# Mixed expert units with the weights stationary: first layer of a full tile and a half tile as one moving operand of 384 columns

## The chip, the cores and the metric

The kernel runs on one core of a Trainium2 chip. The metric is the device time of one execution in microseconds; the time of a kernel is the median of its runs. Engines are named as in the profile: PE is TensorE (PEld its weight loads), DVE VectorE, ACT ScalarE, POOL GpSimd, SP SyncE.

## What is computed

Three blocks follow one another: an attention over clusters of heads, a dense feed-forward block, and a block of 8 experts, all in float32. Only the last is touched by the change:

```
out = x.copy()
do_compute = (x @ w_skip) > 0                  # x: 1536 x 512
e = argmax(x[do_compute] @ w_gate)             # one expert of 8 per token
for e in range(8):
    h = maximum(x[rows of e] @ w1[e], 0)       # w1[e]: 512 x 1024
    y[rows of e] = gate * (h @ w2[e])          # w2[e]: 1024 x 512
out[do_compute] = x + y
```

## The kernel before

Every float32 operand of a matmul is split in two parts, a high one (a cast to fp32r) and a low one (the operand less its high part). A product is three matmuls: high by high, high by low, and low by high. All matmuls in question accumulate in PSUM over the 512 rows of `w1` in four steps `k` of 128, and over the columns of `w1` in two chunks `c` of 512.

The expert block, `moe2`, works through a fixed list of units, the string `TURNS = "01U2UZUVWV"`, numbered 0 to 9; a unit is the tokens that one expert takes at a time. U is two full tiles of 128 tokens, W one full tile, Z and the digits 1 and 2 one half tile of 64, and V one full tile and one half tile, 192 tokens in all. Units 7 and 9 are V, unit 8 between them is W. A section for more units than these stands behind a branch that these inputs don't take.

Per unit the work is this. `gather` brings the tokens' rows by an indirect DMA; `transx` (lines 1233 to 1246) turns them on PE into PSUM tiles `pt`, and ACT and DVE make the high and the low part of `xT`. `first(t, c)` (line 1269) makes 512 columns of the hidden layer for tile `t`. For the units U it calls `wide`, which keeps the weights stationary and lets 256 tokens move, so that the hidden layer comes out already turned. For all other units the tokens are stationary and 512 weight columns move (`group`, line 1202): 12 matmuls of 128x512 for a full tile, 8 for a half tile, whose high and low parts share one stationary operand of 128 columns. The result `h` (two PSUM buffers in the pool of that name) is read out by ACT into `hb` (line 1279), turned back by PE in `transh` (line 1300 for a full tile, line 1296 with the matrix `two`, which also adds the two halves, for a half tile), and split again by ACT and DVE into `hT`. `second` multiplies `hT` by `w2`, into `yo`.

The weights of a unit are four chunks of 128x2048, loaded by DMA into `raw` or `even`; `ahead` takes one of five slots (`wh` and `wl`, `lasth` and `lastl`) as soon as its last reader is done, casts the chunk on ACT (`hi`, line 1541) and subtracts on DVE (`lo`, line 1545). The order of all this is that of the Python code: each engine takes its instructions in the order in which `run` emits them. `run` walks a list of turns `(t, c)`: all first layers of a unit, then its second layers. Before a one-tile unit's second layer one first layer of the next unit is put. In a turn, `ahead` stands in front of the matmuls, and the `transh` of one turn comes after the matmuls of the next; for the units U (`w`), `transh` follows at once and `ahead` comes after it.

Of the kernel before, what the change touches and what calls it, by code (L numbers as in the profile page):

```python
# [20 lines left out]
P = 128  # L21
# [1158 lines left out]
def moe2(ctx, tc, A, cst, R, y1d, wsp, wk, op, ps, x0, route, room):  # L1180
# [6 lines left out]
    xs = x0[1][2]  # L1187
# [24 lines left out]

    left = {(n, c): len(u) for n, u in enumerate(UNIT) for c in range(NPC)}
# [6 lines left out]
    def is_half(t):  # L1220
        return TILES[t][2] < P
# [4 lines left out]

    def side(t):
        return slice(UNIT[TILES[t][0]].index(t) * P, (UNIT[TILES[t][0]].index(t) + 1) * P)
# [4 lines left out]
    def transx(t):  # L1233
        n = TILES[t][0]
        pt = ps["t"].tile([P, 4, P], F32, tag="t", name="pt")
        if is_half(t):
            xT[t] = [xs]
            transpose_half(nc, ident, xg[t], pt, xs, TILES[t][1])
            return
        if is_wide(n):  # L1240
            if t == UNIT[n][0]:
                xT[n, "wide"] = [both("xT", 2) for _ in "hl"]
            xT[t] = [x[:, :, side(t)] for x in xT[n, "wide"]]
        else:
            x = both("xT", 2)
            xT[t] = x[:, :, :P], x[:, :, P:]
        transpose_x(nc, ident, xg[t], pt, *xT[t])
# [20 lines left out]

    def first(t, c, ks=range(4)):
        n = TILES[t][0]  # L1270
        if is_wide(n):
            return wide(t, c)
        if ks[0] == 0:
            hp[t, c] = ps["h"].tile([P, DM], F32, tag="h", name="h")
        group(hp[t, c], xT[t], wsp.w[n, c], is_half(t), True, True, ks)
        if ks[-1] == KD - 1:
            done(n, c)
            r = wk.tile([P, DM], F32, tag="hb", name="hb")
            nc.scalar.activation(r, hp.pop((t, c)), AF.Copy if is_half(t) else AF.Relu)
            hb[t, c] = r  # L1280

    def transh(t, c, late=None):
        r = hb.pop((t, c))
        if is_wide(TILES[t][0]):
            return r()
# [28 lines left out]
    def second(t, c, which=range(3)):  # L1314
        n = TILES[t][0]
        if c == 0 and which[0] == 0:
            yo[t] = ps["y"].tile([P, DM], F32, tag="y", name="yo")
# [98 lines left out]
    def run(n0, n1, fresh=False):  # L1416
# [40 lines left out]
        for t, c in turns:  # L1457
            n = TILES[t][0]
            w = c < 2 and is_wide(n)
# [16 lines left out]
            if c < 2 and n + 1 < n1:  # L1476

                if len(tiles[n]) == 1:
                    rows = tiles[n + 1] if is_wide(n + 1) and c == 0 else () if is_wide(n + 1) else tiles[n + 1][c:c + 1]
# [69 lines left out]
def kernel(ctx, tc, A):  # L1549
# [169 lines left out]
    def more():  # L1719
# [10 lines left out]
        def last():  # L1730
# [4 lines left out]
            return (xT[:, 0], xT[:, 1]), *(x[1][:, o:o + 4 * P].rearrange("p (k m) -> p k m", k=DM // P) for o in (2048, 2048 + 4 * P))  # L1735
# [90 lines left out]
```

## Time and profile before

| | us |
|---|---|
| runs shown, median of 3 | 719.35 (719.34, 719.35, 721.04) |
| profiled execution, its own time | 718.92 |
| its span, first to last instruction | 717.1 |
| first matmul of unit 7 | 652.84 |
| first matmul of unit 8 | 674.56 |
| last matmul's start group, then the last output and its scatter | 707.80, 708.93, 709.96 |

The profile is one execution on the chip. A busy share is an average over the whole span; what a change in one stage is worth is read in that stage's timeline. There, a row is a run of like instructions of one engine: when it begins, how long it is busy, how many there are, and in brackets how long the engine was idle before and who ended that. Consecutive matmuls overlap, so their cost is taken from one start to the next and not from the busy time. The rows themselves are in the section ahead of the prediction.

### The profile page before, as it was taken

The numbers are of one execution on the slowest core, as the hardware profiler recorded it, in microseconds if no ns is written. First come the engines' busy times: TensorE is split into PE (matmuls) and PEld (weight loads), VectorE is DVE, ScalarE is ACT, GpSimd is POOL, SyncE is SP. The second block draws the span as 40 slices with busy tenths as digits, with TensorE's granted clock in tenths as the row PEclk, the third lists the DMA queues.
The fourth block names the chain that finished last, engine by engine and source line by source line (L and its number), as shares of the span: only waits on it lengthen the run. The fifth ranks groups of instructions, "written<-read, shape, count | busy, mean of one in ns | idle before, by whom it ended". The sixth has DMA issues, their size and how long they took to land.

```text
span 717.1 us, 11778 instructions
## 1 busy us (share of the span) xinstructions
PE 699.9 (98%) x4111; PEld 625.8 (87%) x4111; DVE 568.2 (79%) x1114; ACT 472.1 (66%) x905; POOL 381.9 (53%) x339
## 2 busy tenths in 40 slices
PE   8999999999999999999999999999999999999995
PEld 5998989989999899888889999999888989898884
DVE  6989988898989878788784989976468888785651
ACT  6889788888889954554545655556645867574640
POOL 4659779697896386666662000001025888884201
PEclk9999999999999999999999999999999999999998
DMA  7867666676765133333203600026444999996000
GB/s 204 213 160 177 133 166 157 156 173 127 169 164 123 41 115 122 133 138 136 119 1 122 188 0 1 1 64 202 147 149 139 385 367 320 353 352 262 33 10 25
DMA packets 43904, 108.42 MB, mean 151 GB/s; under 512 B 8698, under 2 KB 24522, under 8 KB 38464
## 3 DMA queue, kind: packets, MB, share of 16 engines
q1 hardware_dynamic: 36768, 67.03, 34.4%
q0 software_dynamic: 7072, 40.60, 15.3%
q8 instruction: 34, 0.56, 0.3%
q14 instruction: 30, 0.25, 0.1%
HBM read 74.78 MB, written 10.10 MB: 118 GB/s over the span
## 4 chain that ended last, share of the span: by engine, by line
PE 66%; DVE 8%; DMA 8%; ACT 6%; POOL 6%; issue 5%; POOLq 0%; SPq 0%; ACTq 0%; DVEq 0%
PE h L677 18%; PE y L726 16%; DMA raw<-in_wall_dram,wi 7%; PE yo L1210 5%; PE pt L342 4%; PE hw L1263 4%; PE h L1210 3%; PE s L308 2%; PE px L360 2%; DVE nm L324 2%; PE y L736 2%; ACT e L331 2%; PE s L311 2%; DVE etl L345 2%; PE px L362 2%
## 5 line engine op out<-in xcount | busy, mean ns | idle before, releaser
L345 DVE TENSOR_TENSOR etl<-pt,eth 128x384 fp32r<-128x384 f32 x192 | 101.9, 549 | 19.6 <-ACT eth L344 18.4
L344 ACT CAST eth<-pt 128x384 fp32r<-128x384 f32 x192 | 90.9, 485 | 19.4 <-PE pt L342 19.4
L1177 POOL DMA_INDIRECT xg<-y1d,gi x16 | 27.8, 1738 | 130.5 <-DVE gi L1026 113.8
L342 PE MATMUL pt<-ident,e 128*128 128x128 f32 x576 | 93.8, 272 | 0.3 <-ACT e L331 0.3
L331 ACT ACTIVATE e<-s,nm 128x768 f32<-128x768 f32 x96 | 87.4, 910 | 6.4 <-DVE nm L324 5.6
L324 DVE TENSOR_REDUCE nm<-s 128x1 f32<-128x768 f32 x96 | 90.5, 943 | 0.9 <-PE s L311 0.8
L705 ACT CAST gh<-gm 128x384 fp32r<-128x384 f32 x60 | 30.8, 513 | 81.8 <-DVE gm L703 58.5
L342 PEld LDWEIGHTS pt<-ident,e 128*128 128x128 f32 x576 | 73.6, 140 | 7.0 <-ACT e L331 0.6
L707 DVE TENSOR_TENSOR gl<-gm,gh 128x384 fp32r<-128x384 f32 x60 | 49.4, 824 | 25.7 <-ACT gh L705 25.7
L360 PE MATMUL px<-etl,vh 128*64 128x384 f32 (+1 forms) x192 | 65.5, 368 | 1.5 <-DVE etl L345 1.3
L308 PE MATMUL s<-AB 128*128 128x384 f32 x192 | 57.5, 381 | 2.5 <-ACT e L331 2.1
L577 POOL TENSOR_TENSOR pre<-ct,pre 128x512 int32<-128x512 int32 x26 | 37.2, 1451 | 35.8 <-DVE ct L575 35.8
L677 PE MATMUL h<-xh,wh 128*128 128x384 f32 x256 | 55.6, 338 | 0.6 <-DVE gm L700 0.4
L677 PE MATMUL h<-xh,wl 128*128 128x384 f32 x256 | 56.0, 339 | 0.0
L677 PE MATMUL h<-xl,wh 128*128 128x384 f32 x256 | 55.0, 336 | 0.0
L362 PE MATMUL px<-eth,vh 128*128 128x384 f32 x160 | 54.0, 337 | 0.0
L1545 DVE TENSOR_TENSOR wl<-raw,wh 128x2048 fp32r<-128x2048 f32 (+2 forms) x26 | 44.5, 1717 | 11.7 <-ACT wh L1541 11.7
L311 PE MATMUL s<-CD 128*128 128x384 f32 x192 | 49.3, 338 | 1.0 <-DVE CD L439 1.0
L677 PEld LDWEIGHTS h<-xh,wh 128*128 128x128 f32 x256 | 45.5, 188 | 3.3 <-DVE gm L700 0.5
L677 PEld LDWEIGHTS h<-xh,wl 128*128 128x128 f32 x256 | 44.6, 188 | 2.7 <-POOL wl L649 2.6
L677 PEld LDWEIGHTS h<-xl,wh 128*128 128x128 f32 x256 | 45.7, 188 | 0.0
L1541 ACT CAST wh<-raw 128x2048 fp32r<-128x2048 f32 (+2 forms) x26 | 37.4, 1444 | 10.6 <-PE yo L1210 10.6
(357 smaller groups left out, 1816.8 us busy)
## 6 DMA issues: line engine op xcount, KB each, us to landing
AB<-RL SPq DMA_DIRECT2D x31, 384.0 KB, 5.3
raw<-in_w_in_dram SPq DMA_DIRECT2D x16, 512.0 KB, 4.0
raw<-in_w_out_dram SPq DMA_DIRECT2D x16, 512.0 KB, 4.7
raw<-in_wall_dram SPq DMA_DIRECT2D x8, 1024.0 KB, 8.2
Tp<-in_qkT_dram SPq DMA_DIRECT2D x16, 384.0 KB, 4.1
CD<-RL SPq DMA_DIRECT2D x15, 384.0 KB, 6.9
raw<-in_wall_dram POOLq DMA_DIRECT2D x4, 1024.0 KB, 11.8
vt<-in_v_dram SPq DMA_DIRECT2D x8, 384.0 KB, 6.3
```

Of the source, the lines that this page charges most:

```text
L308: nc.tensor.matmul(s[:, u, :384], lhsT=AB[:, 0, t * P:(t + 1) * P], rhs=AB[:, 1, ks], start=True, stop=False)
L311: nc.tensor.matmul(s[:, u, :384], lhsT=CD[:, 0, t * P:(t + 1) * P], rhs=CD[:, 1, ks], start=False, stop=True)
L324: nc.vector.tensor_reduce(out=nm, in_=s[:, :, :384], axis=AX.XY, op=ALU.max, negate=True)
L331: nc.scalar.activation(e.rearrange("p (u c) -> p u c", u=2), s[:, :, :384], AF.Exp, bias=nm, accum_out=den[:, i % 3:i % 3 + 1])
L342: nc.tensor.transpose(pt[:, i2], e[:, kt * P:(kt + 1) * P], ident)
L344: nc.scalar.copy(eh, pt)
L345: lows[u] = lambda: nc.vector.tensor_tensor(out=etl[:, 3 * u:3 * u + 3, q * P:(q + 1) * P], in0=pt, in1=eh.bitcast(F32), op=ALU.subtract)
L360: nc.tensor.matmul(px[:m], lhsT=vh[:, kt, :m], rhs=etl[:, kt], start=False, stop=False)
L362: nc.tensor.matmul(px, lhsT=vh[:, kt, :], rhs=eth[:, kt], start=False, stop=(kt == NT - 1))
L677: nc.tensor.matmul(hs[c], lhsT=a[:, k * P:(k + 1) * P], rhs=x[:, k, c * HC:(c + 1) * HC], start=(k == 0 and i == 0), stop=(k == KD - 1 and ...
L726: nc.tensor.matmul(ys[gi * GT + t], lhsT=a[:, t * P:(t + 1) * P], rhs=w, start=(f == 0 and n == 0), stop=(gi == 0 and f == NF - 1 and n == 2))
L1210: nc.tensor.matmul(out, lhsT=l[:, k], rhs=r[:, k * DM:(k + 1) * DM], start=start and k == 0 and i == 0, stop=stop and k == 3 and i == len( ...
```

## The change

For units of a full tile and a half tile (`is_mid`: units 7 and 9; unit 0 is left as it is) the first layer is done like that of the units U, by a new function `middle`: the weights are stationary, 128 columns at a time, and the 192 tokens move. The moving operand `xm` holds, for each `k`, 384 columns: 192 high ones (128 of the full tile, 64 of the half one) and then 192 low ones. The high weights meet all 384, the low weights meet the first 256, that is the 192 high ones and 64 of the low ones. In PSUM, columns 0 to 191 so gather high by high and low by high, columns 192 to 383 high by low. ACT copies the second half out (`r`), DVE adds the first half to it (`q`), ACT takes the Relu as the high part, and DVE makes the low parts, laid out in `hm` so that the half tile's high and low part lie side by side for `second`. One call of `middle` makes 256 columns of the hidden layer for all 192 tokens, in two PSUM tiles of 128 columns (`d`), from the pool `h` with its two buffers; a unit takes four calls where it took four calls of `group` before. `transh` makes no PE instruction any more for these units.

`run` treats them like the units U: `transh` follows at once, `ahead` comes behind it, and behind unit 8's first turn both tiles of unit 9 are turned together. `last` gives `xm` a place in the tiles `lasth` and `lastl`, over that of `xs`.

```
@@ moe2 @@
+    class Parts:
+        def __init__(self, m, half, low):
+            o = P if half else 4 * HALF * low
+            self.m, self.s = m, slice(o, o + P)
+        def __getitem__(self, at):
+            k = at[1]
+            return self.m[k // 2][:, k % 2, self.s]
...
+    def is_mid(n):
+        return len(UNIT[n]) == 2 and not is_wide(n) and n > 1
@@ transx @@
+        if is_mid(n):
+            for k in range(KD):
+                nc.tensor.transpose(pt[:, k], xg[t][:, k * P:(k + 1) * P], ident)
+            a, m, b0 = (P, HALF, TILES[t][1]) if is_half(t) else (0, P, 0)
+            for i, x in enumerate(xm):
+                hi, lo, p2 = x[:, :, a:a + m], x[:, :, 3 * HALF + a:3 * HALF + a + m], pt[:, 2 * i:2 * i + 2, b0:b0 + m]
+                nc.scalar.copy(hi, p2)
+                nc.vector.tensor_tensor(out=lo, in0=p2, in1=hi.bitcast(F32), op=ALU.subtract)
+            return
...
+    def middle(t, c):
+        n = TILES[t][0]
+        wh, wl = wsp.w[n, c]
+        i = UNIT[n].index(t)
+        H3 = 3 * HALF
+        hm = both("hT", HT).rearrange("p a b -> p (a b)")[:, :12 * HALF].rearrange("p (d m) -> p d m", d=2)
+        hM.setdefault((n, c), {})[i] = hm
+        r, q = (wk.tile([P, DM], F32, tag="hb", name="hb")[:, :2 * H3].rearrange("p (d m) -> p d m", d=2) for _ in range(2))
+        for d in range(2):
+            h = ps["h"].tile([P, DM], F32, tag="h", name="hm")
+            for k in range(4):
+                o, x = k * DM + (2 * i + d) * P, xm[k // 2][:, k % 2]
+                if k == 3:
+                    nc.tensor.matmul(h[:, :4 * HALF], lhsT=wl[:, o:o + P], rhs=x[:, :4 * HALF], start=False, stop=False)
+                nc.tensor.matmul(h[:, :6 * HALF], lhsT=wh[:, o:o + P], rhs=x, start=k == 0, stop=k == 3)
+                if k < 3:
+                    nc.tensor.matmul(h[:, :4 * HALF], lhsT=wl[:, o:o + P], rhs=x[:, :4 * HALF], start=False, stop=False)
+            nc.scalar.copy(r[:, d], h[:, H3:2 * H3])
+            nc.vector.tensor_tensor(out=q[:, d], in0=h[:, :H3], in1=r[:, d], op=ALU.add)
+        done(n, c)
+        def parts():
+            nc.scalar.activation(hm[:, :, :H3], q, AF.Relu)
+            for a, b, m in ((0, 4 * HALF, P), (P, H3, HALF)):
+                nc.vector.scalar_tensor_tensor(out=hm[:, :, b:b + m], in0=q[:, :, a:a + m], scalar=0.0, in1=hm[:, :, a:a + m].bitcast(F32),
+                                               op0=ALU.max, op1=ALU.subtract)
+        hb[t, c] = parts
...
@@ transh @@
-        if is_wide(TILES[t][0]):
+        if is_wide(TILES[t][0]) or is_mid(TILES[t][0]):
             return r()
@@ second @@
+        if is_mid(n):
+            hT[t, c] = Parts(hM[n, c], is_half(t), 0), Parts(hM[n, c], is_half(t), 1)
...
@@ run @@
-            w = c < 2 and is_wide(n)
+            w = c < 2 and (is_wide(n) or is_mid(n))
...
-                    rows = tiles[n + 1] if is_wide(n + 1) and c == 0 else () if is_wide(n + 1) else tiles[n + 1][c:c + 1]
+                    w1 = is_wide(n + 1) or is_mid(n + 1)
+                    rows = tiles[n + 1] if w1 and c == 0 else () if w1 else tiles[n + 1][c:c + 1]
...
@@ last @@
+            mid = [t[:, 2048:2048 + 6 * P].rearrange("p (k m) -> p k m", k=2) for t in x]
```

On PE, where unit 7 begins, the tokens were stationary (the second name of each pair; `h_7789` is the full tile's PSUM buffer, `h_7804` the half tile's, `lasth` and `lastl` a weight slot's two parts, which also house the tokens' parts), with the turning `pt` behind them:

```order
L1210 MATMUL h_7789<-lasth_6289,xT_7712 128x512 [waits Activation_49]
L1210 MATMUL h_7789<-lasth_6289,xT_7712 128x512 x3
L1210 MATMUL h_7789<-lastl_6290,xT_7712 128x512 x4
L1210 MATMUL h_7789<-lasth_6289,xT_7712 128x512 [waits DVE_49]
L1210 MATMUL h_7789<-lasth_6289,xT_7712 128x512 x3
L1210 MATMUL h_7804<-lasth_6289,lastl_6290 128x512 [waits DVE_49]
L1210 MATMUL h_7804<-lasth_6289,lastl_6290 128x512 x3
L1210 MATMUL h_7804<-lastl_6290 128x512 x4
L1300 MATMUL pt_7815<-ident_63,hb_7802 128x128 [waits Activation_49]
L1300 MATMUL pt_7815<-ident_63,hb_7802 128x128 x3
```

Now it is this, from the fourth PSUM tile of unit 7 into the fifth; `hm_7834` is in the second of the two buffers, `hm_7856` in the first again:

```order
L1309 MATMUL hm_7834<-lasth_6289 128x384 [waits DVE_49]
L1311 MATMUL hm_7834<-lasth_6289,lastl_6290 128x256
L1309 MATMUL hm_7834<-lasth_6289 128x384
L1311 MATMUL hm_7834<-lasth_6289,lastl_6290 128x256
L1309 MATMUL hm_7834<-lastl_6290,lasth_6289 128x384
L1311 MATMUL hm_7834<-lastl_6290 128x256
L1308 MATMUL hm_7834<-lastl_6290 128x256
L1309 MATMUL hm_7834<-lastl_6290,lasth_6289 128x384
L1309 MATMUL hm_7856<-lasth_6289,wh2_6286 128x384 [waits DVE_49]
L1311 MATMUL hm_7856<-lasth_6289,wl2_6287 128x256
```

Eight matmuls of 384 and 256 columns stand for each PSUM tile, no turning is left, and each new tile waits for DVE, since DVE's add is the last reader of the buffer that it takes over.

On ACT in unit 7, the casts of unit 8's first two weight chunks (`even0`, `even1`) stood here, ahead of the reads of `h` and behind the second of them:

```order
L1541 CAST wh4_6537<-even0_5265 128x2048 [waits DMASW1_49,DVE_49,PE_49]
L1279 ACTIVATE hb_7802<-h_7789 128x512 [waits PE_49]
L1279 ACTIVATE hb_7813<-h_7804 128x512 [waits PE_49]
L1301 CAST hT_7816<-pt_7815 128x4x128 [waits DVE_49,PE_49]
L1541 CAST lasth_6289<-even1_6288 128x2048 [waits DMASW7_49,DVE_49]
L1279 ACTIVATE hb_7841<-h_7828 128x512 [waits PE_49,Activation_49]
L1297 ACTIVATE hT_7844<-pt_7843 128x4x64 [waits PE_49]
L1279 ACTIVATE hb_7860<-h_7851 128x512 [waits PE_49,Activation_49]
L1301 CAST hT_7863<-pt_7862 128x4x128 [waits DVE_49,PE_49]
```

They now stand between the calls of `middle`, each behind one call's Relu (line 1317) and ahead of the next call's two copies (line 1312):

```order
L1312 COPY hb_7791<-hm_7793 128x192 [waits PE_49]
L1312 COPY hb_7791<-hm_7804 128x192 [waits PE_49]
L1317 ACTIVATE hT_7790<-hb_7792 128x2x192 [waits DVE_49]
L1600 CAST wh4_6537<-even0_5265 128x2048 [waits DMASW1_49]
L1312 COPY hb_7821<-hm_7823 128x192 [waits PE_49,Activation_49]
L1312 COPY hb_7821<-hm_7834 128x192 [waits PE_49]
L1317 ACTIVATE hT_7820<-hb_7822 128x2x192 [waits DVE_49]
L1600 CAST lasth_6289<-even1_6288 128x2048 [waits DMASW7_49]
L1312 COPY hb_7854<-hm_7856 128x192 [waits PE_49,Activation_49]
L1312 COPY hb_7854<-hm_7867 128x192 [waits PE_49]
L1317 ACTIVATE hT_7853<-hb_7855 128x2x192 [waits DVE_49]
```

What moved is the first cast, behind a copy and a Relu that wait for PE and DVE, and in front of the next call's copies.

On DVE in unit 7 the subtraction for each cast chunk (line 1545) stood among the splits of `hT`, behind unit 6's outputs (line 1338):

```order
L1338 SCALAR_TENSOR_TENSOR xg0_3824<-yo_7739,xg_7160 128x512 [waits DMASW5_49,DMASW4_49,PE_49]
L1545 TENSOR_TENSOR wl4_6538<-even0_5265,wh4_6537 128x2048 [waits DMASW1_49,Activation_49]
L1308 TENSOR_TENSOR hT_7816<-pt_7815,hT_7816 128x4x128 [waits Activation_49]
L1545 TENSOR_TENSOR lastl_6290<-even1_6288,lasth_6289 128x2048 [waits DMASW7_49,Activation_49]
L1305 SCALAR_TENSOR_TENSOR hT_7844<-pt_7843,hT_7844 128x4x64 [waits Activation_49]
L1308 TENSOR_TENSOR hT_7863<-pt_7862,hT_7863 128x4x128 [waits Activation_49]
L1166 TENSOR_TENSOR xT_7871<-pt_7870,xT_7871 128x4x128 [waits Activation_49]
```

Now each one stands between one call's low parts (line 1319) and the next call's adds (line 1313):

```order
L1313 TENSOR_TENSOR hb_7792<-hm_7793,hb_7791 128x192 [waits Activation_49]
L1313 TENSOR_TENSOR hb_7792<-hm_7804,hb_7791 128x192 [waits Activation_49]
L1319 SCALAR_TENSOR_TENSOR hT_7790<-hb_7792,hT_7790 128x2x128 [waits Activation_49]
L1319 SCALAR_TENSOR_TENSOR hT_7790<-hb_7792,hT_7790 128x2x64
L1604 TENSOR_TENSOR wl4_6538<-even0_5265,wh4_6537 128x2048 [waits DMASW1_49,Activation_49]
L1313 TENSOR_TENSOR hb_7822<-hm_7823,hb_7821 128x192 [waits DVE_49,Activation_49]
L1313 TENSOR_TENSOR hb_7822<-hm_7834,hb_7821 128x192 [waits Activation_49]
L1319 SCALAR_TENSOR_TENSOR hT_7820<-hb_7822,hT_7820 128x2x128 [waits Activation_49]
L1319 SCALAR_TENSOR_TENSOR hT_7820<-hb_7822,hT_7820 128x2x64
L1604 TENSOR_TENSOR lastl_6290<-even1_6288,lasth_6289 128x2048 [waits DMASW7_49,Activation_49]
L1313 TENSOR_TENSOR hb_7855<-hm_7856,hb_7854 128x192 [waits DVE_49,Activation_49]
```

The adds, for which PE's next PSUM tile waits, have moved behind a subtraction that waits for the ACT cast of the same chunk.

## Rows read from the trace of the kernel before

**Rows 1.** Stretches of the last units: busy us by engine, clock, DMA share, GB/s.
```profile
660.00:680.00 20.00, 20.00 (x102) 16.68 (x101) 13.55 (x12) 12.02 (x14) 4.87 (x3) 1.00 0.07 28
680.00:700.00 20.00, 20.00 (x105) 16.70 (x104) 10.88 (x10) 9.40 (x14) 1.24 (x2) 1.00 0.04 12
```

**Rows 2.** Timeline of PE, units 7 and 8: start, busy us, line, operation, count.
```profile
655.64 1.09 PE L1210 MATMUL h<-lasth,lastl 128*128 128x512 f32 x4
656.57 1.08 PE L1210 MATMUL h<-lastl 128*128 128x512 f32 x4
657.49 0.60 PE L1300 MATMUL pt<-ident,hb 128*128 128x128 f32 x4
657.84 1.17 PE L1210 MATMUL h<-wh,xT 128*128 128x512 f32 x4
658.85 1.09 PE L1210 MATMUL h<-wl,xT 128*128 128x512 f32 x4
...
660.72 1.00 PE L1296 MATMUL pt<-two,hb 128*128 128x64 f32 x8
661.52 1.17 PE L1210 MATMUL h<-wh,lastl 128*128 128x512 f32 x4
...
707.80 1.10 PE L1210 MATMUL yo<-wh,hT 128*128 128x512 f32 x4
```

**Rows 3.** Timeline of PE, matmuls of 256 columns (unit 6's kind), then of 384 (feed-forward).
```profile
600.83 1.11 PE L1263 MATMUL hw<-xT,wh 128*128 128x256 f32 x8
601.78 0.64 PE L1263 MATMUL hw<-xT,wl 128*128 128x256 f32 x4
...
400.02 0.85 PE L677 MATMUL h<-xh,wl 128*128 128x384 f32 x4
400.71 0.85 PE L677 MATMUL h<-xh,wh 128*128 128x384 f32 x4
```

**Rows 4.** Timeline of ACT, then of DVE, in unit 7.
```profile
653.04 1.91 ACT L1541 CAST wh<-even 128x2048 fp32r<-128x2048 f32 x1 [3.56 <-PE yo L1210]
657.69 0.60 ACT L1279 ACTIVATE hb<-h 128x512 f32<-128x512 f32 x1 [1.25 <-PE h L1210]
658.18 0.58 ACT L1301 CAST hT<-pt 128x512 fp32r<-128x512 f32 x1
...
654.98 2.29 DVE L1545 TENSOR_TENSOR wl<-even,wh 128x2048 fp32r<-128x2048 f32 x1 [1.19 <-ACT wh L1541]
658.79 0.69 DVE L1308 TENSOR_TENSOR hT<-pt,hT 128x512 fp32r<-128x512 f32 x1 [1.52 <-ACT hT L1301]
```

**Rows 5.** Groups by line and shape: busy us, mean ns, idle before and its releaser.
```profile
L1297 ACT ACTIVATE hT<-pt 128x256 fp32r<-128x256 f32 x9 | 3.5, 389 | 6.4 <-PE pt L1296 6.4
L344 ACT CAST eth<-pt 128x384 fp32r<-128x384 f32 x192 | 90.9, 485 | 19.4 <-PE pt L342 19.4
L195 DVE TENSOR_TENSOR eq<-sim,mx 128x192 f32<-128x192 f32 x14 | 5.0, 358 | 0.9
L1263 PEld LDWEIGHTS hw<-xT,wh 128*128 128x128 f32 x192 | 24.6, 189 | 0.3
```

**Rows 6.** Timeline at the kernel's start: DVE, then PE behind a wait.
```profile
13.71 0.95 DVE L439 CAST CD<-RL 64x1536 fp32r<-64x1536 f32 x1
14.80 0.59 PE L311 MATMUL s<-CD 128*128 128x384 f32 x2 [1.01 <-DVE CD L439]
15.23 0.51 PE L308 MATMUL s<-AB 128*128 128x384 f32 x2
```

**Rows 7.** Stretches with a changing clock, at the start and behind the last matmul.
```profile
8.00:9.00 1.00, 0.46 (x3) 0.07 (x1) 0.96 (x3) 0.36 (x1) 0.85 (x1) 0.76 0.70 154
9.00:10.00 1.00, 0.88 (x4) 0.55 (x5) 0.93 (x4) 0.34 (x1) 0.00 (x0) 0.50 0.97 194
11.00:12.00 1.00, 1.00 (x5) 0.49 (x4) 0.00 (x0) 0.00 (x0) 0.00 (x0) 0.53 1.02 378
...
711.00:712.00 1.00, 0.00 (x0) 0.00 (x0) 0.00 (x0) 0.00 (x0) 0.00 (x0) 0.83 0.50 193
```

More of the change, by code (lines that the diff above doesn't have):

```diff
@@ L1186, in moe2 @@
         xg[t], xT[t] = x0[0][t], (x0[1][0], x0[1][1:2])[t]
-    xs = x0[1][2]
+    xs, xm = x0[1][2:]
     def gather(t):
@@ L1211, in group @@
                                  start=start and k == 0 and i == 0, stop=stop and k == 3 and i == len(todo) - 1)
+    hM = {}
+    class Parts:
[5 more added lines that the diff above has]
+            return self.m[k // 2][:, k % 2, self.s]
     left = {(n, c): len(u) for n, u in enumerate(UNIT) for c in range(NPC)}
@@ L1272, in first @@
             return wide(t, c)
+        if is_mid(n):
+            return middle(t, c)
         if ks[0] == 0:
@@ L1315, in second @@
         n = TILES[t][0]
+        if is_mid(n):
+            hT[t, c] = Parts(hM[n, c], is_half(t), 0), Parts(hM[n, c], is_half(t), 1)
         if c == 0 and which[0] == 0:
@@ L1734, in last @@
             xT = x[0][:, 2048:].rearrange("p (i k m) -> p i k m", i=2, k=DM // P)
-            return (xT[:, 0], xT[:, 1]), *(x[1][:, o:o + 4 * P].rearrange("p (k m) -> p k m", k=DM // P) for o in (2048, 2048 + 4 * P))
+            mid = [t[:, 2048:2048 + 6 * P].rearrange("p (k m) -> p k m", k=2) for t in x]
+            return (xT[:, 0], xT[:, 1]), *(x[1][:, o:o + 4 * P].rearrange("p (k m) -> p k m", k=DM // P) for o in (2048, 2048 + 4 * P)), mid
         def even(c):
```

## The prediction

> **What bounds the kernel now.** I read the stretches of the last units first, then the timeline of PE there, then those of ACT and DVE, which feed it. From 660 to 700 us PE is busy 20.00 of every 20.00 us at the full clock, while DVE has 13.6 and 10.9 us of work and ACT 12.0 and 9.4 [rows 1]. In the timeline no row of PE from unit 7 on has idle time before it, up to the last group of matmuls at 707.80 [rows 2]. So in this stage the end is set by PE's instruction stream alone, and ACT and DVE hide behind it. A PE instruction taken out is worth its full time, as long as PE doesn't begin to wait. Behind the last matmul come one output and its scatter, which the change leaves alone.
>
> **Part 1: the turnings that go.** Each unit loses four of them, for two tiles and two chunks. For the full tile, the four turnings at 657.49 hold the next matmuls back until 657.84, 0.35 us, and these four then take 1.01 us to the next start instead of the 0.93 that four matmuls of 512 take undisturbed (655.64 to 656.57): 0.43 us in all [rows 2]. For the half tile, the eight instructions at 660.72 cost 0.80 us up to 661.52 [rows 2], and I take the same 0.08 behind them, 0.88 us. Twice each makes 2.62 us a unit, 5.24 us for units 7 and 9. The turning of the tokens stays: four matmuls per tile, before and after.
>
> **Part 2: the matmuls.** Before, a unit's first layer is 2 x (12 + 8) = 40 matmuls of 512 columns at 0.93/4 = 0.233 us: 9.34 us. After, it is 4 calls x 2 tiles x 4 steps = 32 of 384 and 32 of 256 columns, the same 20,480 columns. Those of 256 run at 0.95/8 = 0.119 us, those of 384 at 0.69/4 = 0.173 us in the feed-forward block [rows 3]. There 512 columns are about 2% faster than here, so I take 0.1745: 32 x (0.1745 + 0.119) = 9.38 us, 0.04 more per unit. The bounds are 0.173 and 0.180, that is -0.1 to +0.3 us for both units. Gain of parts 1 and 2: 5.2 us.
>
> Each unit also loads weights 64 times where it did 40 times. The rows of 256 columns each have a load of their own, busy 189 ns, and still follow one another every 119 ns [rows 3, 5]: loads hide behind matmuls. [...]
>
> **Part 3: what PE waits for now.** This is new, and the trace of before has no such wait; I build it from rows. One call of `middle` fills two PSUM tiles of 4 x (0.1745 + 0.119) = 1.17 us each, and the pool has two buffers. So a tile may begin when the tile two before it has been read by an ACT copy and then a DVE add. Behind each of unit 7's first two calls stand, in order: two copies and adds, Relu, the cast of a weight chunk (1.91 us) and its subtraction (2.29 us) [rows 4]. The next call's copies are queued behind the cast on ACT, and its adds behind the subtraction on DVE; PE's third call waits for these adds.
>
> Sizes: a copy of 192 columns lies below the 0.389 us of 256, I take 0.32; an add of 192 columns is 0.36; the Relu of 384, 0.485 [rows 5]. Steps: ACT begins 0.19 us after the last matmul would hand over to the next (656.57 + 0.93 to 657.69), DVE 0.03 us after ACT's end (654.95 to 654.98, 658.76 to 658.79), an engine's next instruction some 0.1 us before the nominal end of the one before (658.18 after 657.69 + 0.60) [rows 2, 4]. From DVE's end to the matmul it took 0.14 us once (14.66 to 14.80) [rows 6]; I take 0.1.
>
> With zero at unit 7's first matmul: tiles 1 and 2 end at 2.34, tiles 3 and 4 at 4.69. Copy 2.53 to 2.85, add to 3.24, Relu 3.27 to 3.76, cast 3.65 to 5.56, subtraction 5.59 to 7.88, the add for tile 3 7.80 to 8.16. Tile 5 begins at 8.26 instead of 4.69: **3.57 us of waiting**. Then tile 4's add to 8.44, Relu 8.47 to 8.95, cast 8.84 to 10.75, subtraction 10.78 to 13.07, add to 13.35; tile 7 begins at 13.45 instead of 10.60: **2.85 us**. No cast follows within the last two calls. Sum 6.4 us. The bounds of the sizes (copy 0.28 to 0.38, Relu 0.40 to 0.55, add 0.30 to 0.40) move it by 0.3 either way, and by far the most of it is the two casts and two subtractions, which have rows.
>
> Unit 9 goes better: its three chunks still to be cast come before or right behind its first call, and unit 8's second layer (24 matmuls, 5.6 us) lies between. Following the same steps through units 8 and 9, DVE is late once: the last subtraction can begin only when unit 8's first second-layer chunk frees its slot, and it and unit 8's output come before the add for the next call: 0.6 us. Behind the very last call, Relu and low parts end 0.3 us after PE has the half tile's first chunk done. Together 0.9 us; bounds 0.3 and 1.5. After each of these four waits PE's first matmuls run slowly: the two behind the wait at 14.80 took 0.43 us to the next start, against 0.35 [rows 3, 6]. That is 0.08 each, 0.3 in all.
>
> Other additions cost nothing on the path. ACT and DVE get four short reads of `pt` where there were two, for each tile that is turned; the first matmuls on them come several us later, behind unit 6's or within unit 8's work, and if that cover were gone, two more reads for each of two tiles, of 0.389 us at most [rows 5], would cost up to 1.6 us a unit. No DMA is added, and POOL and SP are passed by in their old order.
>
> **Sum.** -5.2 + 6.4 + 0.9 + 0.3 = +2.4 us. On the profiled execution's own 718.92 (span 717.1 and 1.8 around it) that is 721.3; the median of the runs shown lies 0.43 above that execution, so the forecast is **721.7 us**, 0.3% slower.
>
> **Rivals.**
> *The waits are much smaller.* If ACT and DVE had the reads done before tiles 5 and 7 need them, only the gain would be left: 719.35 - 5.2 = 714.1. For it speaks the spare time of both engines [rows 1]; against it, the order, in which the reads stand behind the casts. It decides the sign: below 5.2 us of waiting the change is faster. Chance 0.07. A weaker form, in which steps of mine are too long or the small instructions cheaper, so that some 5 to 6 us of waiting remain, gives 719.2 to 720.6. Chance 0.15.
>
> *The clock falls in a wait.* PE stood still from about 708.9 us (707.80 + 1.10), and the granted clock fell before 712 [rows 2, 7]. At the start it was at half from about 8.5 to 11.9 us: 0.76 in the stretch from 8, in which PE was busy 0.46 us, then 0.50, and 0.53 in the stretch from 11 [rows 7]. Waits of 3.6 and 2.9 us with 2.4 us of matmuls between are of this size. A fall behind the first wait would cost next to nothing, since tiles 5 and 6 at half rate end at about 13, within the second wait. [...] Chance 0.17. [...]
>
> *Weight loads are paid for.* [...] The rows of 256 columns are this very pattern and show none of it. Chance 0.03.
>
> **How the numbers follow.** Forecast 0.58 (720.6 to 722.6), smaller waits 0.15, no waits 0.07, clock 0.17, loads 0.03. The range leaves out the last, no waits, and the tails of the others: 719.0 to 723.8. A difference of 0.3%, 2.2 us, is about what a measurement of this kernel can tell from no change. Slower by more than it, above 721.5: some 0.35 of the forecast's 0.58, the clock and the loads, 0.55. Within it: the rest of the forecast and the weak waits, 0.38. Faster: 0.07.
>
> **What would show it.** Unit 7's matmuls of 384 and 256 columns should come in pairs of 0.29 us, with idle PE, released by DVE's add, ahead of its fifth and seventh PSUM tile only, of about 3.6 and 2.9 us. The stretch from unit 7's first matmul to unit 8's first should grow by some 4 us, and that from there to the last matmul shrink by some 1.5. No turning of `hb` should be left in units 7 and 9. The prediction is wrong if ACT's casts don't come between the calls as ordered, if the pairs take 0.32 us or more, or if the granted clock leaves 1.00 before PE's end.

## The result

The changed kernel takes 724.71 us (median of five runs, 723.08 to 727.15) against 719.35 (five, 717.52 to 721.04): **1.0082 times the time before, 95% interval 1.0057 to 1.0106**. The forecast was 721.7 with a range up to 723.8. The direction was right and the size was not: +5.4 us came out where +2.4 was expected.

The profiled execution took 724.71 us with a span of 722.9, against 718.92 and 717.1 before. Up to unit 7 the two traces agree: its first matmul begins at 652.75, before at 652.84 [rows 2]. All of the difference lies behind. Three marks cut it into two stretches: unit 7's first matmul, unit 8's first matmul, and the start of the last four matmuls (707.80 before [rows 2]). Runs of one kernel differ by some 3 us ahead of unit 7 (it begins between 651.4 and 655.1 us in the traces of this study, and the kernel before has runs about 718.3 and about 721), so these stretches tell more than the totals, and I use them throughout. Each is read from the one profiled execution of its kernel.

| us | unit 7 | units 8 and 9 | together |
|---|---|---|---|
| before | 674.56 - 652.84 = 21.72 | 707.80 - 674.56 = 33.24 | 54.96 |
| forecast | some 25.7 | some 31.7 | 57.4 |
| after | 680.22 - 652.75 = 27.47 | 713.59 - 680.22 = 33.37 | 60.84 |

So unit 7 is 1.8 us over the forecast and the rest 1.65. The stretches that answer to [rows 1] show that PE no longer works all the time and that its clock is no longer full. Columns are: stretch, its length, busy time of PE, PEld, DVE, ACT and POOL, granted clock, DMA share, GB/s.

```profile
660.00:680.00 20.00, 18.43 (x76) 16.22 (x77) 12.48 (x18) 8.81 (x11) 1.03 (x2) 0.74 0.04 14
680.00:700.00 20.00, 18.29 (x99) 15.49 (x98) 15.27 (x19) 12.73 (x18) 3.57 (x3) 1.00 0.05 16
```

The timeline of PE after: start, busy us, line, operation; in brackets the idle time before and what ended it.

```profile
652.75 0.33 PE L1309 MATMUL hm<-lasth 128*128 128x384 f32 x1
652.93 0.28 PE L1311 MATMUL hm<-lasth,lastl 128*128 128x256 f32 x1
653.05 0.34 PE L1309 MATMUL hm<-lasth 128*128 128x384 f32 x1
...
661.00 0.69 PE L1309 MATMUL hm<-lasth,wh 128*128 128x384 f32 x1 [3.40 <-DVE hb L1313]
...
661.71 0.52 PE L1309 MATMUL hm<-lasth,wh 128*128 128x384 f32 x1
...
662.24 0.52 PE L1309 MATMUL hm<-lastl,wh 128*128 128x384 f32 x1
...
666.21 0.69 PE L1309 MATMUL hm<-lasth,wh 128*128 128x384 f32 x1 [0.57 <-DVE hb L1313]
...
688.07 0.34 PE L1309 MATMUL hm<-lastl,wh 128*128 128x384 f32 x1
689.12 0.44 PE L1309 MATMUL hm<-lasth,wh 128*128 128x384 f32 x1 [0.72 <-ACT hb L1335]
...
698.55 0.34 PE L1309 MATMUL hm<-lastl,wh 128*128 128x384 f32 x1
699.89 0.44 PE L1309 MATMUL hm<-lasth,wh 128*128 128x384 f32 x1 [1.00 <-DVE hb L1313]
...
705.63 1.10 PE L1210 MATMUL yo<-lastl,hT 128*128 128x512 f32 x4
706.97 1.17 PE L1210 MATMUL yo<-wh,hT 128*128 128x512 f32 x4 [0.24 <-DVE hT L1319]
```

A pair of 384 and 256 columns takes 0.30 us from 652.75 to 653.05, as forecast. Unit 7's PSUM tiles are numbered 1 to 8, two to a call of `middle`. The first wait is where it was expected: tile 5 begins 661.00 - 652.75 = 8.25 us after unit 7's start, forecast 8.26. Behind it a pair takes 0.53 us (661.71 to 662.24), 1.8 times as long. The reason is in the clock:

```profile
658.00:660.00 2.00, 0.00 (x0) 0.00 (x0) 1.61 (x1) 0.79 (x3) 0.00 (x0) 0.99 0.65 262
660.00:662.00 2.00, 0.99 (x3) 1.00 (x4) 1.41 (x4) 0.75 (x2) 0.00 (x0) 0.50 0.03 8
...
668.00:670.00 2.00, 2.00 (x9) 2.00 (x9) 0.36 (x1) 0.32 (x1) 0.00 (x0) 0.50 0.00 0
670.00:672.00 2.00, 2.00 (x13) 1.81 (x12) 0.40 (x2) 0.92 (x3) 0.00 (x0) 0.95 0.00 0
```

The granted clock fell to 0.50 while PE stood still, and stayed there from about 660.0 to about 670.2 us, through tiles 5 to 8. ACT and DVE did what the steps said, to within some 0.1 us of their forecast times from 652.75 on (cast at 3.72, forecast 3.65; subtraction at 5.64, forecast 5.59). ACT's rows first, then DVE's; they answer to [rows 4]:

```profile
656.47 1.89 ACT L1600 CAST wh<-even 128x2048 fp32r<-128x2048 f32 x1
658.26 0.53 ACT L1312 COPY hb<-hm 128x192 f32<-128x192 f32 x2
...
658.39 2.29 DVE L1604 TENSOR_TENSOR wl<-even,wh 128x2048 fp32r<-128x2048 f32 x1 [1.17 <-ACT wh L1600]
660.60 0.61 DVE L1313 TENSOR_TENSOR hb<-hm,hb 128x192 f32<-128x192 f32 x2
```

In unit 9 stands a wait that no step had: 0.72 us, released by ACT's reading of unit 8's `h` (L1335). The rows of ACT and then of DVE there:

```profile
683.72 0.26 ACT L1258 CAST lasth<-pt 128x128 fp32r<-128x128 f32 x1
685.37 0.27 ACT L1258 CAST lastl<-pt 128x128 fp32r<-128x128 f32 x1 [1.39 <-DVE lasth L1259]
...
686.40 0.37 ACT L1258 CAST lastl<-pt 128x256 fp32r<-128x256 f32 x1 [0.49 <-DVE lasth L1259]
686.67 1.91 ACT L1600 CAST wh<-raw 128x2048 fp32r<-128x2048 f32 x1
688.47 0.60 ACT L1335 ACTIVATE hb<-h 128x512 f32<-128x512 f32 x1
...
682.84 2.29 DVE L1604 TENSOR_TENSOR wl<-even,wh 128x2048 fp32r<-128x2048 f32 x1 [0.34 <-ACT wh L1600]
685.05 0.28 DVE L1259 TENSOR_TENSOR lasth<-pt,lasth 128x128 fp32r<-128x128 f32 x1
```

ACT's second read of `pt` writes another tile than the first; with DVE's subtraction it shares nothing but `pt`, which both read. Still it waits for that subtraction, which is queued behind one of 2048 columns: ACT stands 1.39 and then 0.49 us, the cast of unit 9's second chunk slides behind, and behind the cast the read of `h` that PE waits for. Why two reads of one tile wait for each other, no run here shows.

### The profile page after: what moved, and what is told of

Read it like the earlier page. It is cut to its first block, busy times and chain, and to the rows that moved or that the text cites. A ratio compares the mean times of both kernels' runs of the same rounds, so it can differ in the third digit from the quotient of the medians.

```text
span 722.9 us, 11814 instructions
## 1 busy us (share of the span) xinstructions
PE 700.0 (97%) x4111; PEld 628.0 (87%) x4111; DVE 574.6 (79%) x1142; ACT 473.3 (65%) x917; POOL 380.7 (53%) x339
## 4 chain that ended last, share of the span: by engine, by line
PE 71%; DVE 9%; ACT 7%; POOL 5%; issue 4%; DMA 2%; SPq 1%; POOLq 0%; another core or an unknown queue 0%; ACTq 0%; DVEq 0%
PE h L677 18%; PE y L726 15%; PE yo L1210 9%; PE hw L1288 5%; PE pt L342 4%; PE h L1210 3%; PE s L308 2%; PE px L360 2%; ACT e L331 2%; PE y L736 2%; PE s L311 2%; DVE nm L324 2%; DVE etl L345 2%; PE px L362 2%; PE sim L188 2%
## 5 line engine op out<-in xcount | busy, mean ns | idle before, releaser
L707 DVE TENSOR_TENSOR gl<-gm,gh 128x384 fp32r<-128x384 f32 x60 | 49.4, 824 | 25.7 <-ACT gh L705 25.7
L726 PE MATMUL y<-wh,gh 128*128 128x512 f32 x168 | 43.6, 393 | 0.0
```

The lines of the kernel that those rows point to most:

```text
L726: nc.tensor.matmul(ys[gi * GT + t], lhsT=a[:, t * P:(t + 1) * P], rhs=w, start=(f == 0 and n == 0), stop=(gi == 0 and f == NF - 1 and n == 2))
```

## The experiments

The theory after the result: (1) unit 7's loss is the ring of two PSUM buffers behind the casts, and a clock that falls in its first wait; (2) unit 9's is the turns that ACT and DVE take on `pt`; (3) the matmuls themselves gained what was forecast. The main rival: the new pattern of matmuls and weight loads is slower in itself, or ACT and DVE are simply too slow for it. Ratios are against runs of the kernel before on the same chip; they are estimated from all runs of both and are not exactly the quotient of the two medians.

**The waits filled with dummy matmuls.** PE gets more work, none of it used.

```
+FILLN = (20, 16)
...
+        if n == 7 and c == 1:
+            yd = ps["y"].tile([P, DM], F32, tag="y", name="fill")
+            for _ in range(FILLN[i]):
+                nc.tensor.matmul(yd[:, :6 * HALF], lhsT=xm[0][:, 0, :P], rhs=xm[0][:, 0], start=True, stop=True)
         for d in range(2):
             h = ps["h"].tile([P, DM], F32, tag="h", name="hm")
```

> Adds idle work to PE and changes nothing else: 20 matmuls of 384 columns ahead of unit 7's fifth PSUM tile and 16 ahead of its seventh, into a PSUM tile that nobody reads. At 0.1745 us each they take 3.49 and 2.79 us, just under the waits of 3.57 and 2.85 that the sum had. Theory (half of the loss in unit 7 is the clock, which falls while PE waits): the granted clock stays at 1.00, the stretch from unit 7's first matmul to unit 8's first goes from 27.5 us to about 25.6, and the kernel with more work takes about 722.8 us, 1.9 less than the change as it is. Rival (the clock is a bystander, the loss is the waits alone): the stretch stays at 27.5 and the time at 724.7 or above.

Measured: 722.60 us, ratio 1.0047 [1.0028, 1.0066]; unit 7 25.68 us, together 59.01. The timeline of PE, then the clock:

```profile
659.75 3.63 PE L1307 MATMUL fill<-lasth 128*128 128x384 f32 x20
665.73 2.94 PE L1307 MATMUL fill<-lasth 128*128 128x384 f32 x16
```
```profile
660.00:665.00 5.00, 5.00 (x31) 4.75 (x30) 3.45 (x5) 2.54 (x5) 0.16 (x1) 1.00 0.39 157
```

Thirty-six matmuls more make unit 7 1.8 us shorter than in the changed kernel: with PE busy the clock stays at 1.00. The 25.68 us is what the steps gave for unit 7 without a fall (21.72 - 2.62 + 0.04 + 6.4 + 0.16 = 25.7). So, in these two traces, the two causes in unit 7 part cleanly: 4.0 us of waiting net of the gain, 1.8 us of clock.

**Only the first wait filled.** The same edit with `FILLN = (20, 0)`.

> Twenty dummy matmuls of 384 columns fill the first wait of unit 7, and the second wait is left empty. Theory (a wait of some 3 us lets the clock fall, and the first one does it): the first wait keeps full clock, the second is 2.8 us and may let the clock fall behind it, for the last two tiles and the second layer: unit 7 25.7 us without a fall, 26.5 to 28 with one. Rival (the fall came from what lay before the wait, not from the empty TensorE): the clock falls at 660 as in the changed kernel, filled or not.

Measured: 726.47 us (721.57 to 726.70), ratio 1.0102 [1.0075, 1.0129]. The profiled execution is the fastest of them: unit 7 25.65, rest 33.34. PE, then the clock:

```profile
664.84 0.44 PE L1314 MATMUL hm<-lasth,wh 128*128 128x384 f32 x1 [2.62 <-DVE hb L1318]
```
```profile
665.00:670.00 5.00, 5.00 (x30) 4.57 (x31) 2.03 (x7) 2.95 (x5) 0.00 (x0) 1.00 0.00 0
```

Here the second wait shows at its full size, 2.62 us, and in this execution no fall follows it. The other four runs took 724.26 to 726.70 us with a mean clock of 0.992 to 0.994, the profiled one 0.997; that the clock fell behind the second wait there fits, but without traces of them it is not shown, and the clock alone need not make up all of their 5 us. The rival (a cause that lies ahead of the wait) finds no support: with the first wait filled the clock was 1.00 from 655 to 675.

**Unit 9 alone, and unit 7 alone.** In the first only unit 9 has the new first layer, in the second only unit 7.

```
-        return len(UNIT[n]) == 2 and not is_wide(n) and n > 1
+        return n == 9
```

> The change for unit 9 alone, unit 7 as before. Theory (unit 9 earns 2.6 us of turnings and gives 2.5 back in waits of its own, for reads of one PSUM tile that ACT and DVE take in turn and for the last casts): no difference to before within 0.3 us, about 719.4, with three waits of PE of about 0.7, 1.0 and 0.2 us as in the change. Rival (unit 9's waits are left over from unit 7's delay): the waits are smaller and the time about 717.9.

Measured: 718.53 us, ratio 0.9993 [0.9974, 1.0011]; unit 7 21.72, rest 33.33 (before 33.24). Waits 0.72, 0.94 and 0.25. Unit 9 gains nothing: what its turnings gave goes into waits.

```
+        return n == 7
```

> The change for unit 7 alone, unit 9 as before. Theory: all of the loss is here, +5.7 us, about 725.1, with a wait of about 3.4 us ahead of the fifth PSUM tile and the clock at half behind it for some 10 us. Rival (the loss is spread over both units): about 722.

Measured: 727.27 us (723.03 to 729.52, four runs), ratio 1.0115 [1.0087, 1.0144]. In the profiled execution, the fastest of the four, units 8 and 9 take 33.23 us, as before, so its loss is unit 7's. The other three took 4.1 to 6.5 us longer at nearly the same mean clock (0.990 against 0.991). What made them longer is not shown, and the median lies 2.2 us above the 725.1 expected. PE and the clock of the profiled one:

```profile
666.06 0.45 PE L1309 MATMUL hm<-lasth,wh 128*128 128x384 f32 x1 [1.23 <-DVE hb L1313]
```
```profile
660.00:665.00 5.00, 3.98 (x16) 3.72 (x16) 3.25 (x6) 2.76 (x4) 1.17 (x1) 0.66 0.14 55
665.00:670.00 5.00, 3.94 (x25) 3.75 (x26) 2.62 (x7) 1.89 (x6) 0.00 (x0) 1.00 0.00 0
```

In this execution the clock fell behind the same wait of 3.40 us, but was back before 665: tiles 5 and 6 ran slowly, the second wait took that in (1.23 us left of 2.62), and unit 7 took 25.67 us, as if nothing had happened. This is the case that the prediction had called "next to nothing". The fall comes, then, in every trace with this wait (the changed kernel, this one, and the paired reads below); its length does not repeat.

**The casts behind the calls.** The two casts of unit 8's weights are issued after unit 7's four calls.

```
-            if use and wsp.slots and w:
+            if is_mid(n) and n == 7 and c < 2:
+                while use and wsp.slots and (t, c) == (tiles[n][-1], 1):
+                    ahead()
+            elif use and wsp.slots and w:
                 ahead()
```

> The casts and subtractions for unit 8's and 9's chunks are held back until unit 7's four calls are through, so that none stands between the calls; same work. Theory (the casts between the calls make the waits, and the waits make the clock fall): no wait over 0.3 us in unit 7, clock 1.00, the stretch from unit 7's first matmul to unit 8's first 19.1 to 19.6 us, 8 less than in the change, and a total of 717 to 718.5, since ACT and DVE are then later in unit 9 by up to 1 us. Rival (two PSUM buffers are too few whatever stands between): waits of a microsecond or more remain in unit 7, and the time stays above 720.

Measured: 719.68 us, ratio 1.0000 [0.9983, 1.0017]. Unit 7: 19.56 us, full clock, and no row of PE with idle time before it: without the casts between the calls both waits are gone. But the rest grew to 35.66 us, and the expected gain over before was missed. PE from tile 4 into tile 5, then the timeline of DVE, then of PE in unit 9:

```profile
657.42 0.34 PE L1309 MATMUL hm<-lastl,lasth 128*128 128x384 f32 x1
657.90 0.44 PE L1309 MATMUL hm<-lasth,wh 128*128 128x384 f32 x1
```
```profile
677.45 2.28 DVE L1607 TENSOR_TENSOR wl<-even,wh 128x2048 fp32r<-128x2048 f32 x1
```
```profile
681.01 0.44 PE L1309 MATMUL hm<-lasth,wh 128*128 128x384 f32 x1 [1.52 <-DVE lasth L1259]
683.71 0.45 PE L1309 MATMUL hm<-lasth,wh 128*128 128x384 f32 x1 [0.98 <-ACT hb L1335]
```

DVE now does five subtractions of 2048 columns between 666 and 680 us, and the short reads for unit 9's tiles stand behind them. The wait moved from unit 7 to unit 9.

**Unit 9's reads in pairs.** Both ACT copies of `pt` are issued before both DVE subtractions.

```
-            for i, x in enumerate(xm):
-                hi, lo, p2 = x[:, :, a:a + m], x[:, :, 3 * HALF + a:3 * HALF + a + m], pt[:, 2 * i:2 * i + 2, b0:b0 + m]
+            ps2 = [(x[:, :, a:a + m], x[:, :, 3 * HALF + a:3 * HALF + a + m], pt[:, 2 * i:2 * i + 2, b0:b0 + m]) for i, x in enumerate(xm)]
+            for hi, lo, p2 in ps2:
                 nc.scalar.copy(hi, p2)
+            for hi, lo, p2 in ps2:
                 nc.vector.tensor_tensor(out=lo, in0=p2, in1=hi.bitcast(F32), op=ALU.subtract)
```

> Only the order of the four reads of pt for unit 9's tiles changes: both ACT copies are issued before both DVE subtractions, so that the two engines no longer take turns on one PSUM tile. Theory (the turns are what made unit 9's waits 2.4 us instead of 0.9): the second cast of unit 9 starts about 1.4 us earlier, the wait of 0.69 to 0.72 us ahead of tile 15's first matmul goes, about 0.6 and 0.4 us of waits stay, and the stretch from unit 8's first matmul to the last group of four falls from 33.4 to 31.9 us. Rival (the reads cost nothing, the lateness comes from the DVE's subtraction of 2048 columns alone): the stretch stays at 33.2 to 33.4 us. Unit 7 is as in the changed kernel, 25.7 us without a fall of the clock and up to 27.5 with one. Time: 1.5 us under the changed kernel by the theory, the same by the rival.

Measured: 723.26 us, ratio 1.0048 [1.0028, 1.0068]; units 8 and 9 in 32.14 us instead of 33.37. ACT's rows, then the two waits of PE that stay:

```profile
683.65 0.26 ACT L1258 CAST lasth<-pt 128x128 fp32r<-128x128 f32 x1
683.80 0.28 ACT L1258 CAST lastl<-pt 128x128 fp32r<-128x128 f32 x1
...
684.51 1.94 ACT L1601 CAST wh<-raw 128x2048 fp32r<-128x2048 f32 x1
```
```profile
698.56 0.45 PE L1310 MATMUL hm<-lasth,wh 128*128 128x384 f32 x1 [0.67 <-DVE hb L1314]
...
705.65 1.17 PE L1210 MATMUL yo<-wh,hT 128*128 128x512 f32 x4 [0.25 <-DVE hT L1320]
```

No idle time is left between the reads, the cast comes at 684.51 instead of 686.67, and the wait of 0.72 us is gone. Two waits stay, 0.67 and 0.25 us in the brackets. Counted as the prediction counts, from the start of the matmuls before (697.55 and 704.31) less the 0.17 and 0.93 us that these take, they cost 0.84 and 0.41 us, where the prediction had 0.6 and 0.3. This settles the second cause: 1.2 us. In unit 7, which the edit leaves alone, the clock fell again behind 3.40 us of waiting, from about 661.0 to 671.3. That is into the second layer, and unit 7 took 28.48 us, 1 us over the 27.5 that had been set as its upper end.

**More buffers, the order left alone.** Unit 7's calls of `middle` take their PSUM tiles from the pools `h`, of two buffers, and `t`, of three, in turn.

```
-            h = ps["h"].tile([P, DM], F32, tag="h", name="hm")
+            tag = "ht"[i if n == 7 else 0]
+            h = ps[tag].tile([P, DM], F32, tag=tag, name="hm")
```

> Unit 7's two tiles take their PSUM from two pools in turn (the two buffers of h, the three of t) instead of from h alone; no instruction is moved, and the casts of unit 8's weights stay between the calls. Theory (the waits are those for a ring of two buffers, whose reads stand behind a cast of 1.9 us and a subtraction of 2.3 us): the waits of 3.4 and 2.8 us inside the first layer go, up to 2.2 us of them comes back where the second layer waits for the last parts on DVE, unit 7 takes 21.6 us (before 21.72, changed 25.7 to 27.5), and the clock does not fall at 660. Rest 33.4 to 34.1. Time: level with the kernel before, within 1.5 us. Rival (ACT and DVE are simply too slow for unit 7, with any number of buffers): unit 7 stays above 24 us and the time above 722.

Measured: 720.66 us, ratio 1.0022 [1.0003, 1.0041]. Unit 7 20.53 us with one wait left:

```profile
668.68 0.73 PE L1210 MATMUL yo<-wh,hT 128*128 128x512 f32 x2 [0.97 <-ACT hT L1318]
```

With the casts in their old place and no instruction moved, both waits inside the first layer are gone. So they need both, casts between the calls and a ring of two buffers, and either cure removes them. That ACT and DVE are too slow for unit 7 is refuted. The rest took 36.31 us, more than the 33.4 to 34.1 expected: with unit 7 shorter DVE is late for unit 9, as with the casts held (waits of 1.06 and 0.98 us), and the clock fell behind those two:

```profile
684.00:686.00 2.00, 2.00 (x9) 1.92 (x9) 2.00 (x2) 0.41 (x2) 0.00 (x0) 0.50 0.00 0
```

**Everything, with POOL's help.** Both pools, the paired reads, and three subtractions of 2048 columns on POOL; the pairs in the edit are unit and weight chunk.

```
-            wsp.lo(n, c, nc.vector)
+            wsp.lo(n, c, nc.gpsimd if (n, c) in ((8, 1), (8, 3), (9, 3)) else nc.vector)
```

> The change with its three covers gone: unit 7's tiles from two pools in turn, unit 9's four reads of pt in pairs, and the subtractions of 2048 columns for three of the eight casts, (8,1), (8,3) and (9,3), on POOL instead of DVE (POOL takes 1.45 us for 512 columns, so some 5.8 us each, on an engine that has waits of 14 us here). Theory (the matmuls are 5.2 us shorter as forecast and everything else was waiting for buffers and for DVE): unit 7 19.6 us, the rest 31.4 to 32.0, together 51 to 51.6 us against 54.96 before: 3.4 to 4 us faster than before, 715.3 to 717. Rival (DVE and POOL slow each other, or another wait takes the place): the rest stays at 33 or more and the time at 718 or above.

Measured: 720.52 us, ratio 1.0017 [0.9995, 1.0039]: a miss, and the first half of the rival is the reason, as far as DVE goes: those of its instructions with two SBUF inputs that begin while POOL subtracts take longer. Unit 7 took 23.13 us, the rest 32.43. The timelines of DVE and POOL, then of PE, then the clock:

```profile
666.93 3.73 DVE L1321 SCALAR_TENSOR_TENSOR hT<-hb,hT 128x256 fp32r<-128x256 f32 x2 [0.59 <-ACT hT L1319]
...
684.10 3.48 DVE L1606 TENSOR_TENSOR wl<-raw,wh 128x2048 fp32r<-128x2048 f32 x1 [1.04 <-ACT wh L1602]
...
665.57 4.61 POOL L1606 TENSOR_TENSOR lastl<-even,lasth 128x2048 fp32r<-128x2048 f32 x1 [6.60 <-ACT lasth L1602]
...
680.78 4.65 POOL L1606 TENSOR_TENSOR wl<-even,wh 128x2048 fp32r<-128x2048 f32 x1
```
```profile
672.00 1.22 PE L1210 MATMUL yo<-wh,hT 128*128 128x512 f32 x2 [2.09 <-ACT hT L1319]
```
```profile
672.00:674.00 2.00, 2.00 (x5) 1.61 (x6) 0.84 (x3) 2.00 (x2) 0.00 (x0) 0.50 0.30 115
```

While POOL subtracts (665.57 to 670.18), two DVE instructions that read two SBUF tiles take 3.73 us instead of 0.63; they end 0.5 us after POOL does. At 684.10 a DVE subtraction takes 3.48 instead of 2.29 us, with POOL busy until 685.43. DVE's short reads of `pt`, with one input in PSUM, ran in between at their usual length (0.28 to 0.42 us, as in the changed kernel). So POOL's help is not free: 3.1 us on DVE, 2.1 us of them a wait of PE, and a fall of the clock behind it. In both cases POOL had begun first.

**Both pools and paired reads, without POOL.** The two edits shown above, together.

> Two things of the runs before together, and nothing on POOL: unit 7's tiles from two PSUM pools in turn (measured alone: unit 7 in 20.5 us instead of 27.5, one wait of 1.0 us left ahead of the second layer) and unit 9's reads of pt in pairs (measured alone: the rest in 32.1 us instead of 33.4). Theory (two separate causes, which add): unit 7 20.5, the rest 31.9 to 32.2, together 52.4 to 52.7 against 54.96 before, and no wait longer than 1 us, so full clock throughout: 2.3 to 2.5 us faster than before. Rival (the shorter unit 7 leaves DVE late for unit 9, as it did where the casts were held back): the rest 33.5 or more, together 54 or more, level with before.

Measured: 717.47 us, ratio 0.9983 [0.9965, 1.0001]; unit 7 20.54, rest 32.91, together 53.45: 1.5 us better than before in these stretches, full clock; the interval of the ratio still touches 1. The two cures add, less 0.8 us. That is a new wait, for DVE's part of unit 9's tokens, ahead of unit 9's first PSUM tile (0.56 us idle, 0.8 from start to start).

**And the second cast behind the calls**, with the transposes of tile 13, the tokens of unit 8, ahead of it.

```
+            seven = n == 7 and (t, c) in F[7][1:]
+            if seven and (t, c) == (tiles[n][-1], 1):
+                transx(tiles[n + 1][0])
+                while use and wsp.slots:
+                    ahead()
-            if use and wsp.slots and w:
+            elif use and wsp.slots and w and not seven:
                 ahead()
...
-                for t2 in rows:
+                for t2 in () if seven else rows:
```

> As the run with both pools and the paired reads, and the second cast of unit 8's weights is issued behind unit 7's four calls, with tile 13's transposes ahead of it. Theory (what is left of the wait ahead of the second layer is that cast and its subtraction): unit 7 19.3 to 19.6 us, the rest 32.5 to 32.9 with a wait of 0.9 ahead of tile 15 since DVE is later, together 52.0 to 52.4: 0.3 us better than without the move at most, 2.6 to 3 us faster than before. Rival (a held cast only moves the wait, as it did alone): together 52.6 or more.

Measured: 716.57 us (715.03 to 718.35, 12 runs) against 718.68: ratio **0.9961 [0.9946, 0.9975]**. Unit 7 19.28, rest 32.99, together 52.27 against 54.96 before. The gain over the run without the move, 1.2 us, is larger than the 0.3 expected, since the wait ahead of the second layer went and the rest hardly grew. What is left of PE's waits:

```profile
678.56 0.44 PE L1311 MATMUL hm<-lasth,wh 128*128 128x384 f32 x1 [0.64 <-DVE lasth L1260]
...
690.18 0.44 PE L1311 MATMUL hm<-lasth,wh 128*128 128x384 f32 x1 [0.68 <-DVE hb L1315]
...
697.26 1.17 PE L1210 MATMUL yo<-wh,hT 128*128 128x512 f32 x4 [0.25 <-DVE hT L1321]
```

This version beats the kernel before, by 0.4%, and the changed one: 1.6 us of waits instead of 5.9 and no fall of the clock.

## Why the prediction was right and wrong

**Parts 1 and 2, turnings and matmuls: right.** Forecast gain 2.58 us a unit. With the waits out of the way unit 7 took 19.56 and 19.28 us against 21.72: 2.2 to 2.4. The pairs came in at 0.30 us with 64 weight loads a unit, and no load showed in the time, so the rival of paid loads fell; the chances count it above 721.5 us, with a price of a load that no run shows. The missing 0.1 to 0.4 us lies in handovers too short to show as idle time. With the casts held, tile 5 began 0.48 us after the start of tile 4's last matmul (657.42 to 657.90) instead of 0.17, and its own first matmul took 0.28 us to the next start (658.18) instead of 0.17: 0.4 in all. In the last version tile 7's two are 0.22 and 0.28: 0.16.

**Part 3, unit 7's waits: right in place, releaser and size.** First wait: tile 5 began 8.25 us after the start, forecast 8.26. Without a fall of the clock unit 7 took 25.68 and 25.65 us in the two filled kernels, and 25.67 where the clock was back before the second wait ended; the forecast was 25.7. The two edits that remove the mechanism (other buffers; casts elsewhere) removed the waits.

**The clock: the first step that failed.** The prediction had it as a rival of 0.17 and wrote that a fall behind the first wait "would cost next to nothing, since tiles 5 and 6 at half rate end at about 13, within the second wait". Tiles 5 and 6 did end there (661.00 + 4.6 = 665.6, and the second wait shrank to 0.57 us). What failed is the length. Had it been the 3.4 us of the kernel's start [rows 7], the clock would have been back before tile 7. In the changed kernel it stayed at half for some 10.2 us, through tiles 7 and 8 too, which took 4.25 us (666.21 to 670.46) instead of 2.35. That is the 1.8 us by which the changed kernel's unit 7 stands over the filled one. The one execution in which the clock came back before 665 lost nothing, just as the step said. The step was not wrong about every fall, but it took the clock to be back for tile 7, and the length varies. The chances put this rival above 721.5 us, with a cost that no row of before shows; the runs showed 1.8 us in the changed kernel, 2.8 with the paired reads (28.48 against 25.68) and nothing in that one execution. A clock that leaves 1.00 before PE's end was also one of the prediction's own signs of being wrong, and it came. The chance was too low as well: the clock fell behind 3.40 us of waiting in all three traces that have this wait, and the mean clock of the five runs was 0.985 to 0.991, against 0.993 to 0.998 before.

**Unit 9: the second step that failed.** "Other additions cost nothing on the path" was said of the four short reads of `pt`, because the matmuls on them come several us later. The step looked for who needs the reads and not for what is queued behind them. ACT and DVE take turns on `pt`, DVE's turn is behind a subtraction of 2.29 us, and ACT's next cast is behind that. Counted as the prediction counts, from the start of the matmul before less the 0.17 us that it takes (0.93 for the last group), the waits cost 0.88, 1.17 and 0.41 us, 2.46 in all, instead of 0.9. The brackets show only 1.96, since busy times of consecutive matmuls overlap (652.75 + 0.33 against the next start at 652.93). Issued in pairs they cost 1.25 and the stretch lost 1.2 us. Another 0.35 of the 1.65 is the two late waits, 0.84 and 0.41 instead of 0.6 and 0.3. The last 0.1 stays open. The price that the prediction named for the reads without their cover, up to 1.6 us a unit, was of the right size, though the cost came by the queue and not by the matmuls on them.

**The sum.** Forecast +2.4 on the profile; measured 60.84 - 54.96 = +5.9. Of the 3.5 between them 1.8 is the clock and 1.65 units 8 and 9, of which 1.2 is the turns on `pt` and 0.35 the late waits that were forecast too short.

## What to carry to other kernels

Work taken off a PE that never waits is worth its time only as far as the buffers that PE fills come free as fast (here unit 7 went from 21.72 to 27.47 us, and to 19.28 with those waits gone); find what stands ahead of their readers in ACT's and DVE's queues, and try another pool before you move work, since holding the casts back only moved the wait to the next unit (35.66 us for units 8 and 9 instead of 33.24). Of any new operand that two engines read from PSUM, look at what is queued behind each read as well as at who uses it (here the queue cost 1.2 us). A wait of PE of the size seen here should be priced with a fall of the clock behind it, which in these traces lasted from 3.4 to 10.2 us.

## What the runs showed of the hardware

- The clock fell to 0.50 behind single waits of 3.40 us (three of three traces) and 2.09 us (one), and behind 1.06 and 0.98 us that lay 2.7 us apart (one); it stayed at 1.00 behind 2.62 us in one trace, and behind 1.52 and 0.98 us, also 2.7 us apart, in another. Three of these five falls lasted some 3.4 us (660.5 to 663.9 with unit 7 alone, 683.9 to 687.3 with both pools, 671.9 to 675.3 with POOL's help) and two some 10.2 (660.0 to 670.2 in the changed kernel, 661.0 to 671.3 with the paired reads); the last of these came 1.1 us after PE had begun again.
- 36 dummy matmuls in PE's two waits made unit 7 1.8 us shorter (25.68 instead of 27.47), with the clock at 1.00 from 650 to 715.
- POOL's subtraction of 128x2048 took 4.6 to 4.9 us, and the DVE instructions with two SBUF inputs that began while one ran took longer: two of them 3.73 us instead of 0.63, one 3.48 instead of 2.29, and two more, at 696.82, 1.53 instead of 0.63. They ended 0.48, 2.15 and 0.49 us after POOL did.
